# Keys for the estimate of the softmax maximum: column tiles in fp32 over 16 keys a head, against the whole array in fp32r over 32

## The chip, the cores and the metric

The kernel runs on one core of a Trainium2 chip. The metric is the time of one execution on the device in microseconds; of the kernel before, three runs gave 940.66 us (median; 939.57 to 941.91). The profile is one further execution of the same program. In it PE is TensorE's matmul, PEld its weight load, DVE VectorE, ACT ScalarE, POOL GpSimd and SP SyncE.

## The reference

For 2048 tokens of width 448 the reference mixes, by a gate for each token, an attention branch (16 heads of 28, one shared set of keys and values) and an MLP branch that shifts tokens against each other.

```
g = sigmoid((x * gate_w).sum(-1))
q = (x @ wq) in 16 heads of 28;  k = x @ wk;  v = x @ wv
p = softmax(q @ k.T * 28 ** -0.5)          # over all 2048 keys
a = (p @ v, heads side by side) @ wo
h  = gelu(layernorm(x) @ w1), its four quarters shifted by +1, -1, +2, -2 tokens
x1 = x + h @ w2
b  = x1 + gelu(layernorm(x1) @ w3) @ w4
out = g * a + (1 - g) * b
```

A softmax has the same value whatever number is taken off all scores of a row, as long as no exponential overflows. The kernel uses that: it takes off not the maximum over all 2048 keys, but the maximum over the first few.

## The kernel before

The kernel works in three stages: projections and the shifted mixing (to about 165 us), the w3/w4 MLP (to 401 us), and attention with the output projection (to the end). All five engines take their instructions in the order in which the code is written; nothing is sorted afterwards.

The attention stage is cut into 16 units. Unit u holds four heads (their 28 query rows lie at partitions 0, 32, 64 and 96) of one block of 512 tokens. A unit has eight steps (`i` from 0 to 7), each over two tiles of 128 keys. In one step the instructions of TensorE stand in this order:

- twelve score products for the first key tile, then twelve for the second (L204, in `scores`). Each works on a row tile of the array, 32 rows x 128 columns, and streams 512 queries as fp32r; four of them, one a head, run side by side. The results go to two single PSUM banks and a bank pair for each key tile.
- the value products of the step before (L868, in `values`): column tiles of 128 rows x 32 columns, fp32, four side by side, one a head. They write to the bank `s0`, and, where the step has no other use for it, in two halves to `s0` and `s1`.
- in most steps one or two parts of the output projection (L820, in `by_columns`): column tiles in fp32 as well, 224 columns each.

ScalarE takes the exponentials of the single banks and of the pairs (L857). VectorE copies one pair out of PSUM (L905), adds the values to the sum of the unit (`values_end`, L794) and adds the output projection (L839). The second score group of a step can begin only when the two single banks that the previous step used as `s0` and `s1` are read.

The maxima of the next unit are made in step `i = 2` of a unit (`at_max`, `MAX_AT = 2`), in place of the output projection: the values go whole to `s0`, and `max_part` writes its products to `s1`. There are fifteen such steps, for units 1 to 15. In `max_part` (L206) the stationary operand is the 128 queries of a token tile `t` (all four heads, 128 rows), and the moving operand is `khd`, in which the first `MK` keys stand four times on a block diagonal, so that one product gives `MK` scores for each of four heads. One `reduce_max` on VectorE (L213) then makes 16 maxima for each partition. `max_end`, two steps later, splits them and sends them by DMA into spare rows of the queries, where the score products subtract them.

Unit 0 has its maxima made during the MLP stage: four calls of `max_part`, one token tile each, are dealt out as `fills` between the w4 products (L683 to L685, whole array, fp32r, 448 columns) of block 2.

At the end of the kernel, `check` looks whether a row's sum of exponentials went above `LIMIT` = 1e18; if one did, a branch computes all of attention again with true maxima (`max_full`).

Of the kernel before, what the change touches and what calls it, by code (L numbers as in the profile page):

```python
# [9 lines left out]
F32 = mybir.dt.float32  # L10
F32R = mybir.dt.float32r
# [5 lines left out]
P = 128  # L17
# [12 lines left out]
EPS = 1e-5  # L30
SHIFTS = (-1, 1, -2, 2)
PB = 6
MK = 32
LIMIT = 1e18


def f32(ap):
    return ap.bitcast(F32)
# [3 lines left out]
def gated_mix_kernel(  # L42
# [12 lines left out]
    nc = tc.nc  # L55
# [98 lines left out]
    def layernorm_stats(pool, b):  # L154
        mv, rs = stats_tiles(pool, b)
        for t in range(4):
            stats_tile(pool, b, t, mv)
        stats_end(mv, rs)
        return mv, rs

    def layernorm_norm(b, t, mv, rs, xn, xt4):
        xt = x1[:, 4 * b + t, :]
        nc.vector.tensor_scalar(xn, xt, mv[:, t, 0:1], rs[:, t:t + 1], op0=ALU.subtract, op1=ALU.mult)
        nc.vector.transpose(xt4[:, :, t, :], xn.rearrange("p (f j) -> p f j", j=32))
# [3 lines left out]
    def xt_write(b, xt4):  # L168
        xd_of[b] = dram.tile([NE, 32, 4, 128], F32, tag="xd", bufs=2, name=f"xd_{b}")
        for p in range(4):  # L170
            nc.sync.dma_start(xd_of[b][:, :, p].rearrange("f i u -> i f u"),
                              xt4[32 * p:32 * p + 32].rearrange("i f t j -> i f (t j)"))
# [9 lines left out]
    qr_of, qh_of, ql_of = {}, {}, {}  # L182
# [8 lines left out]
    def q_high(u, qh, ql):  # L191
        qh_of[u], ql_of[u] = qh, ql
        nc.vector.tensor_copy(qh, qr_of[u])
# [12 lines left out]
    def max_part(u, ts, ps):  # L206
        if u not in mx_of:
            mx_of[u] = late.tile([P, 4, 4], F32, tag="mr", bufs=2, name=f"mr_{u}")
        n = len(ts)
        for i, t in enumerate(ts):  # L210
            nc.tensor.matmul(ps[:, i * 4 * MK:(i + 1) * 4 * MK], qh_of[u][:, t * P:(t + 1) * P], khd,
                             start=True, stop=True)
        nc.vector.reduce_max(mx_of[u][:, :, ts[0]:ts[0] + n].rearrange("p j t -> p t j"),  # L213
                             ps[:, 0:n * 4 * MK].rearrange("p (t j k) -> p t j k", t=n, j=4), axis=AX.X)

# [34 lines left out]
    with tc.tile_pool(name="s1b", bufs=1) as s1b, \  # L250
# [319 lines left out]
        s1_stack.close()  # L570

        late = ctx.enter_context(tc.tile_pool(name="late", bufs=1, side="right", reuse_waits="tile"))
        khd = late.tile([P, 4 * MK], F32R, name="khd")
        kh_of.append(late.tile([P, S], F32R, name="kh"))
        qh0 = late.tile([P, 512], F32R, name="qh0")
        ql0 = late.tile([P, 512], F32R, name="ql0")
# [7 lines left out]
        def big(name):  # L584
            return s2a.tile([P, 2048], F32, tag="big", bufs=2, name=name)

        def load_w34(i, pool):
            w3h.append(pool.tile([P, 4, 2 * P], F32R, name=f"w3h_{i}"))
            w3l.append(pool.tile([P, 4, 2 * P], F32R, name=f"w3l_{i}"))
            w4h.append(pool.tile([P, 2, D], F32R, name=f"w4h_{i}"))  # L590
            w4l.append(pool.tile([P, 2, D], F32R, name=f"w4l_{i}"))
            raw = big(f"w34raw_{i}")
            raw3[i] = raw[:, 0:1024].rearrange("p (c n) -> p c n", c=4)
            raw4[i] = raw[:, 1024:1024 + 2 * D].rearrange("p (c n) -> p c n", c=2)
            nc.sync.dma_start(raw3[i], w3[:, :, i * 256:i * 256 + 256])
            nc.sync.dma_start(raw4[i], w4[i * 256:i * 256 + 256, :].rearrange("(c p) n -> p c n", p=P))

        def split_w3(i):
            split_w(raw3[i], w3h[i], w3l[i])

        def split_w4(i):
            nc.scalar.copy(w4h[i], raw4[i])
            nc.vector.tensor_tensor(w4l[i], raw4[i], f32(w4h[i]), ALU.subtract)
# [3 lines left out]
        def ln_read(b):  # L607
            xraw2[b] = big(f"xr_{b}").rearrange("p (c n) -> p c n", c=4)
            xt_read(b, xraw2[b])
# [40 lines left out]
    with tc.tile_pool(name="s2", bufs=1, reuse_waits="tile") as s2, \  # L650
            tc.tile_pool(name="ps2", bufs=1, space=PSUM, reuse_waits="tile") as ps2:
        def weigh_x1(n0, n1):
            for n in range(n0, n1):
                nc.gpsimd.tensor_scalar(x1[:, n, :], x1[:, n, :], gi[:, n:n + 1], None, op0=ALU.mult)
# [4 lines left out]
        def fill():  # L659
            if fills:  # L660
                fills.pop(0)()

        def w3_part(b, f):
            i, k = divmod(f, 2)
            ps = mm_tile(f"g_{b}_{f}")
            proj(ps, w3h[i][:, :, k * P:(k + 1) * P], w3l[i][:, :, k * P:(k + 1) * P], *acts[b])
            if (b, f) == (NB - 1, NF - 1):
                nc.scalar.activation(gf_late, ps, AF.Gelu_apprx_tanh)
                return None
            gh = s2.tile([P, 512], F32R, tag="gh", bufs=3, name=f"gh_{b}_{f}")  # L670
            gl = s2.tile([P, 512], F32R, tag="gl", bufs=3, name=f"gl_{b}_{f}")
            gf = s2.tile([P, 512], F32, tag="gf", bufs=1, name=f"gf_{b}_{f}")
            nc.scalar.activation(gh, ps, AF.Gelu_apprx_tanh)  # L673
            nc.scalar.activation(gf, ps, AF.Gelu_apprx_tanh)  # L674
            nc.vector.tensor_sub(gl, gf, f32(gh))  # L675
            return gh, gl
# [10 lines left out]
        for b in range(NB):  # L687
            acc = [ps2.tile([P, 512], F32, tag="acc", bufs=4, name=f"acc_{b}_{t}") for t in range(4)]
            gs = {}
            for f in range(NF):  # L690
                if f == 9 and b + 1 < NB:
                    mv, rs = layernorm_stats(s2a, b + 1)
                if f == 10 and b + 1 < NB:
                    xt4 = big(f"xt4_{b + 1}")[:, 0:4 * D].rearrange("p (f t j) -> p f t j", f=NE, t=4)
                if f in (10, 11) and b + 1 < NB:
                    for t in (2 * f - 20, 2 * f - 19):
                        xn = s2a.tile([P, 512], F32, tag="xn", bufs=1, name=f"xn_{b + 1}_{t}")[:, 0:D]
                        layernorm_norm(b + 1, t, mv, rs, xn, xt4)
                if f == 11 and b + 1 < NB:
                    xt_write(b + 1, xt4)  # L700
                    ln_read(b + 1)
                gs[f] = w3_part(b, f)
                if b == 0 and f % 2 and f < 11:
                    split_w3((f + 3) // 2)
                    split_w4((f + 3) // 2)
                    if f < 9:
                        load_w34((f + 5) // 2, s2)
                if b == 1 and f == 0:
                    nc.gpsimd.tensor_tensor(gg, invE, gz, ALU.pow)
                    nc.vector.tensor_scalar(gg, gg, 1.0, None, op0=ALU.add)  # L710
                    nc.vector.reciprocal(gg, gg)
                    nc.vector.tensor_scalar(gi, gg, -1.0, 1.0, op0=ALU.mult, op1=ALU.add)
                if b == NB - 1 and f == 4:
                    weigh_x1(0, 4 * b)
                if b == 1 and f == 1:
                    nc.gpsimd.memset(f32(khd), 0.0)
                    for j in range(4):
                        h = slice(32 * j, 32 * j + DH)
                        nc.gpsimd.tensor_copy(khd[h, j * MK:(j + 1) * MK], f32(kh_of[0])[h, 0:MK])
                    qr0 = s2a.tile([P, 512], F32, tag="xn", bufs=1, name="qr_0")  # L720
                    nc.gpsimd.memset(qr0, 0.0)
                    q_load(0, qr0)
                    nc.sync.dma_start(w4_late, w4[F - P:F, :])
                if b == 1 and f == 5:
                    q_high(0, qh0, ql0)
                    q_low(0)
                if f >= 2:
                    for t in range(4):
                        w4_part(f - 2, t, gs[f - 2], acc)
                        if b > 1 and t % 2 == 0 and f < NF - 1:  # L730
                            fill()
            for t in range(4):
                w4_part(NF - 2, t, gs[NF - 2], acc, NF - 2 if b == NB - 1 else NF - 1)
                if b + 1 < NB:
                    ln_split(b + 1, t, t + 1)
            for t in range(4):
                if b < NB - 1:
                    w4_part(NF - 1, t, gs[NF - 1], acc)
                xt = x1[:, 4 * b + t, :]
                nc.vector.tensor_add(xt, xt, acc[t][:, 0:D])  # L740
# [5 lines left out]
    with tc.tile_pool(name="s3", bufs=1, reuse_waits="tile") as s3, \  # L746
# [150 lines left out]
        for c in range(NC):  # L897
            u, i = divmod(c, NT // 2)
# [62 lines left out]
        u = NU - 1  # L961
# [84 lines left out]
        with tc.If(again > 0, label="redo"):  # L1046
            for b in range(NB):
                for g in range(NG):
                    u = b * NG + g
# [6 lines left out]
                    for kt in range(NT):  # L1056
                        ps = [bank(f"s2_{u}_{kt}_{j}") for j in range(4)]
# [4 lines left out]
                        for j in range(4):  # L1062
                            nc.tensor.matmul(pv[32 * j:32 * j + 32, :], vext[:, kt, :], p[:, j],
                                             start=(kt == 0), stop=(kt == NT - 1), tile_position=(0, 32 * j))
# [3 lines left out]
                    for t in range(4):  # L1068
                        ps = bank(f"wo2_{u}_{t}")[:, whole]
# [53 lines left out]
```

## Time and profile before

| | |
|---|---|
| median of three runs | 940.66 us (939.57 to 941.91) |
| profiled execution: time, span | 941.63 us, 939.8 us |
| granted TensorE clock | 0.999 |
| TensorE products of the maxima | 64 (60 in attention, 4 in the MLP stage) |
| reductions of the maxima | 15 of 128 x 512, 4 of 128 x 128 |
| attention stage | from about 401 us to the end |

The time of an execution is the span (first to last instruction) and a little around it, here 1.8 us. A row of the timeline gives start, time to the end, engine, line, operation, the tiles out<-in, and how many instructions are merged; in brackets stands for how long the engine was idle before, and what it waited for. Two shapes are given for a matmul: rows x columns of the stationary operand, and partitions x columns of the moving one. A matmul's end is modelled and lies behind the moment at which the next group can start, so paces are read from starts.

### The profile page before, as it was taken

The numbers are of one execution on the slowest core, as the hardware profiler recorded it, in microseconds if no ns is written. First come the engines' busy times: TensorE is split into PE (matmuls) and PEld (weight loads), VectorE is DVE, ScalarE is ACT, GpSimd is POOL, SyncE is SP. The second block draws the span as 40 slices with busy tenths as digits, with TensorE's granted clock in tenths as the row PEclk, the third lists the DMA queues.
The fourth block names the chain that finished last, engine by engine and source line by source line (L and its number), as shares of the span: only waits on it lengthen the run. The fifth ranks groups of instructions, "written<-read, shape, count | busy, mean of one in ns | idle before, by whom it ended". The sixth has DMA issues, their size and how long they took to land.

```text
span 939.8 us, 22620 instructions
## 1 busy us (share of the span) xinstructions
PE 924.7 (98%) x9573; PEld 618.8 (66%) x9573; DVE 516.5 (55%) x922; ACT 637.4 (68%) x1006; POOL 81.6 (9%) x111
## 2 busy tenths in 40 slices
PE   9999999999999999999999999999999999999997
PEld 6788888888888888855555555555555555555552
DVE  3664264531432431166766666666666666766664
ACT  5542444332222222279999999999999999999994
POOL 3343420200000520020000000000000000000000
PEclk9999999999999999999999999999999999999999
DMA  9822552220300300020000010000011000010001
GB/s 310 288 76 56 168 162 91 50 54 1 84 1 1 84 1 0 1 60 18 19 14 24 13 44 34 24 13 15 23 43 34 15 23 13 27 50 10 8 14 43
DMA packets 40435, 47.24 MB, mean 50 GB/s; under 512 B 10120, under 2 KB 28488, under 8 KB 40328
## 3 DMA queue, kind: packets, MB, share of 16 engines
q1 hardware_dynamic: 37304, 40.27, 14.5%
q10 hardware_dynamic: 3024, 5.47, 1.6%
q8 instruction: 76, 1.25, 0.6%
q14 instruction: 31, 0.25, 0.1%
HBM read 32.56 MB, written 11.67 MB: 47 GB/s over the span
## 4 chain that ended last, share of the span: by engine, by line
PE 92%; ACT 4%; DMA 1%; issue 1%; DVE 1%; SPq 0%; POOL 0%; ACTq 0%; DVEq 0%
PE bank L868 24%; PE bank L204 18%; PE bank L820 5%; PE acc L683 5%; PE acc L685 5%; PE acc L684 5%; ACT p L857 4%; PE g L135 4%; PE g L136 4%; PE g L137 4%; PE pair L204 2%; PE hs L461 1%; PE hs L462 1%; PE g L138 1%; PE g L139 1%; PE h L135 1%
## 5 line engine op out<-in xcount | busy, mean ns | idle before, releaser
L857 ACT ACTIVATE p<-bank 128x512 f32<-128x512 f32 x512 | 265.2, 607 | 25.0 <-PE pair L204 13.9
L868 PE MATMUL bank<-p,vext 128*32 128x256 f32 (+1 forms) x3520 | 245.3, 415 | 4.7 <-ACT p L857 1.3
L868 PEld LDWEIGHTS bank<-p,vext 128*32 128x32 f32 x3520 | 101.4, 109 | 125.8 <-ACT p L857 57.5
L905 DVE COPY p<-pair 128x1024 f32<-128x1024 f32 x127 | 155.5, 1225 | 47.9 <-PE pair L204 39.1
L673 ACT ACTIVATE gh<-g 128x512 fp32r<-128x512 f32 x55 | 32.9, 598 | 183.9 <-PE g L139 183.9
L794 DVE TENSOR_TENSOR o<-o,bank 128x256 f32<-128x256 f32 (+1 forms) x188 | 88.2, 469 | 109.3 <-PE bank L868 76.7
L857 ACT ACTIVATE p<-p 128x1024 f32<-128x1024 f32 x127 | 139.2, 1096 | 0.0
L857 ACT ACTIVATE p<-pair 128x1024 f32<-128x1024 f32 x129 | 136.8, 1060 | 0.0
L675 DVE TENSOR_TENSOR gl<-gf,gh 128x512 fp32r<-128x512 f32 x55 | 38.3, 696 | 166.4 <-ACT gf L674 166.4
L204 PE MATMUL bank<-qh,kh 32*128 32x512 f32 x512 | 125.5, 449 | 0.2 <-DVE ot L839 0.2
L204 PE MATMUL pair<-qh,kh 32*128 32x512 f32 x512 | 118.1, 457 | 0.3 <-DVE x L740 0.3
L204 PE MATMUL bank<-ql,kh 32*128 32x512 f32 x512 | 111.0, 394 | 0.0
L204 PE MATMUL bank<-qh,kl 32*128 32x512 f32 x512 | 108.7, 389 | 0.0
L204 PE MATMUL pair<-ql,kh 32*128 32x512 f32 x512 | 101.0, 389 | 0.0
L204 PE MATMUL pair<-qh,kl 32*128 32x512 f32 x512 | 100.9, 388 | 0.0
L204 PEld LDWEIGHTS bank<-qh,kh 32*128 32x128 f32 x512 | 54.0, 182 | 63.3 <-issue 21.9
L683 PE MATMUL acc<-w4h,gh 128*128 128x448 f32 x220 | 80.3, 365 | 0.0
L685 PE MATMUL acc<-w4h,gl 128*128 128x448 f32 x220 | 80.0, 364 | 0.0
L684 PE MATMUL acc<-w4l,gh 128*128 128x448 f32 x220 | 80.0, 363 | 0.0
L820 PE MATMUL bank<-wof,on 128*32 128x224 f32 (+1 forms) x992 | 67.6, 359 | 0.0
L135 PE MATMUL g<-ah,w3h 128*128 128x512 f32 x168 | 65.8, 392 | 0.0
L136 PE MATMUL g<-al,w3h 128*128 128x512 f32 x168 | 65.7, 391 | 0.0
(199 smaller groups left out, 1418.7 us busy)
## 6 DMA issues: line engine op xcount, KB each, us to landing
qd<-qf ACTq DMA_DIRECT2D x16, 256.0 KB
rb<-rd SPq DMA_DIRECT2D x15, 256.0 KB
x<-in_x_dram SPq DMA_DIRECT2D x4, 896.0 KB
xd<-xt SPq DMA_DIRECT2D x16, 224.0 KB
w34raw<-in_w_dram SPq DMA_DIRECT2D x7, 512.0 KB
qr<-qd SPq DMA_DIRECT2D x64, 56.0 KB
out_dram<-ot SPq DMA_DIRECT2D x15, 224.0 KB
w34raw<-in_w_dram SPq DMA_DIRECT2D x7, 448.0 KB
```

The costliest lines, as they stand in the source:

```text
L135: nc.tensor.matmul(ps, wh[:, c, :], ah[:, c, :], start=(c == 0), stop=False)
L136: nc.tensor.matmul(ps, wh[:, c, :], al[:, c, :], start=False, stop=False)
L204: nc.tensor.matmul(ps[j], k[h, keys], q[h, :], start=(r == 0), stop=(r == 2), tile_position=(32 * j, 0))
L675: nc.vector.tensor_sub(gl, gf, f32(gh))
L683: nc.tensor.matmul(ps, gh[:, tok], w4h[i][:, k, :], start=(f == 0), stop=False)
L684: nc.tensor.matmul(ps, gh[:, tok], w4l[i][:, k, :], start=False, stop=False)
L685: nc.tensor.matmul(ps, gl[:, tok], w4h[i][:, k, :], start=False, stop=(f == stop))
L794: nc.vector.tensor_add(o, o, pv)
L820: nc.tensor.matmul(ps[32 * i:32 * i + 32, :], a[:, c:c + 32], w, start=True, stop=True, tile_position=(0, 32 * i))
L857: nc.scalar.activation(p[:, heads], p[:, heads] if source is None else source, AF.Exp, scale=SCALE)
L868: nc.tensor.matmul(pv[32 * j:32 * j + 32, :], vext[:, kt, :], p_of[k][:, j, qs], start=(k == ks[0]), stop=(k == ks[-1]), tile_position=(0, ...
L905: nc.vector.tensor_copy(pa[:, both], pairs[0])
```

## The change

`MK` goes from 32 to 16, so `khd` has 64 columns instead of 128 and a reduction reads half as many scores. In `max_part` each product of 128 x 128 by 128 columns becomes four products of 128 rows x 32 columns by 64 columns, at the four column tiles, each for 32 tokens. `khd` is stored as fp32 instead of fp32r and the queries are read as fp32; the numbers in them are those that were rounded for fp32r before. The copies that fill `khd` on GpSimd become half as wide. Nothing else is touched; from the second hunk on, lines move down by two.

```
-MK = 32
+MK = 16
...
         for i, t in enumerate(ts):
-            nc.tensor.matmul(ps[:, i * 4 * MK:(i + 1) * 4 * MK], qh_of[u][:, t * P:(t + 1) * P], khd,
-                             start=True, stop=True)
+            for c in range(4):
+                m = t * P + 32 * c
+                nc.tensor.matmul(ps[32 * c:32 * c + 32, i * 4 * MK:(i + 1) * 4 * MK], f32(qh_of[u])[:, m:m + 32], khd,
+                                 start=True, stop=True, tile_position=(0, 32 * c))
...
-        khd = late.tile([P, 4 * MK], F32R, name="khd")
+        khd = late.tile([P, 4 * MK], F32, name="khd")
...
-                    nc.gpsimd.memset(f32(khd), 0.0)
+                    nc.gpsimd.memset(khd, 0.0)
```

On TensorE, in step 2 of unit 0, before the change. `bank_0` and `bank_1` are this step's `s0` and `s1`, `p_0_2` and `p_0_3` the exponentials of key tiles 2 and 3, `qh_1` the queries of unit 1, `qh0` those of unit 0, `kh` the keys; the shape is that of the result:

```order
L868 MATMUL bank_0_3223<-p_0_2_3306,vext_74 32x512 [waits Activation_49]
L868 MATMUL bank_0_3223<-p_0_2_3306,vext_74 32x512 x3
L868 MATMUL bank_0_3223<-p_0_3_3330,vext_74 32x512 x4
L211 MATMUL bank_1_3224<-khd_1043,qh_1_3310 128x128 [waits Activation_49]
L211 MATMUL bank_1_3224<-khd_1043,qh_1_3310 128x128 x3
L204 MATMUL bank_2_3225<-qh0_1045,kh_1044 128x512 [waits Activation_49]
```

The same place after the change:

```order
L870 MATMUL bank_0_3235<-p_0_2_3318,vext_74 32x512 [waits Activation_49]
L870 MATMUL bank_0_3235<-p_0_2_3318,vext_74 32x512 x3
L870 MATMUL bank_0_3235<-p_0_3_3342,vext_74 32x512 x4
L213 MATMUL bank_1_3236<-khd_1043,qh_1_3322 32x64 [waits Activation_49]
L213 MATMUL bank_1_3236<-khd_1043,qh_1_3322 32x64 x15
L204 MATMUL bank_2_3237<-qh0_1045,kh_1044 128x512 [waits Activation_49]
```

Four products became sixteen at the same place, with the same wait; they now have the tile shape of the value products ahead of them.

On TensorE, in block 2 of the MLP stage, before the change (`acc_2_0` and `acc_2_1` are the sums of two token tiles, `m_0_0` the bank for the scores of the first token tile):

```order
L684 MATMUL acc_2_0_2286<-w4l_0_1056,gh_2_0_2302 128x448
L685 MATMUL acc_2_0_2286<-w4h_0_1055,gl_2_0_2303 128x448
L211 MATMUL m_0_0_2347<-khd_1043,qh0_1045 128x128
L683 MATMUL acc_2_1_2287<-w4h_0_1055,gh_2_0_2302 128x448
L684 MATMUL acc_2_1_2287<-w4l_0_1056,gh_2_0_2302 128x448
```

The same place after the change:

```order
L686 MATMUL acc_2_0_2286<-w4l_0_1056,gh_2_0_2302 128x448
L687 MATMUL acc_2_0_2286<-w4h_0_1055,gl_2_0_2303 128x448
L213 MATMUL m_0_0_2347<-khd_1043,qh0_1045 32x64 x4
L685 MATMUL acc_2_1_2287<-w4h_0_1055,gh_2_0_2302 128x448
L686 MATMUL acc_2_1_2287<-w4l_0_1056,gh_2_0_2302 128x448
```

Here four column tiles stand between products that use the whole array.

## The prediction

> **What bounds the kernel now.** I read the page first, then a table by stage, then the timeline around one step with maxima. The page's heads and its chain of work:
>
> ```profile
> span 939.8 us, 22620 instructions
> PE 924.7 (98%) x9573; PEld 618.8 (66%) x9573; DVE 516.5 (55%) x922; ACT 637.4 (68%) x1006; POOL 81.6 (9%) x111
> PE 92%; ACT 4%; DMA 1%; issue 1%; DVE 1%; SPq 0%; POOL 0%; ACTq 0%; DVEq 0%
> ```
>
> TensorE carries 92% of the chain, but ScalarE is nearly full in attention. The table by stretches (length, then busy time of PE, PEld, DVE, ACT, POOL) has the w4 stretch with the four fills, and one attention unit:
>
> ```profile
> 262.00:282.00 20.00, 20.00 (x96) 17.40 (x95) 6.39 (x13) 4.35 (x8) 0.00 (x0) 1.00 0.00 1
> 499.30:531.90 32.60, 32.36 (x492) 17.35 (x488) 22.20 (x40) 31.42 (x50) 0.00 (x0) 1.00 0.07 18
> ```
>
> In the MLP stretch TensorE has no gap. In a unit of 32.6 us ScalarE is idle for 1.2 us, so up to that much can be taken from TensorE before ScalarE bounds. The operations that change (least/median/greatest ns):
>
> ```profile
> L211 PE MATMUL bank<-khd,qh x60: 272/275/328, 414.5 to 870.2; 128*128 128x128 f32 x60
> L213 DVE TENSOR_REDUCE mr<-bank x15: 683/685/686, 415.3 to 870.7; 128x16 f32<-128x512 f32 x15
> L213 DVE TENSOR_REDUCE mr<-m x4: 283/288/294, 274.4 to 279.8; 128x4 f32<-128x128 f32 x4
> ```
>
> The timeline of step 2 of unit 0 and the start of step 3 (unit 0's first step with maxima; the others are within 0.02 us of it):
>
> ```profile
> 413.57 1.04 PE L868 MATMUL bank<-p,vext 128*32 128x512 f32 x8
> ...
> 414.00 0.61 PE L868 MATMUL bank<-p,vext 128*32 128x512 f32 x4
> 414.55 0.52 PEld L211 LDWEIGHTS bank<-khd,qh 128*128 128x128 f32 x4 [0.84 <-ACT p L857]
> ...
> 414.74 0.69 DVE L794 TENSOR_TENSOR o<-o,bank 128x512 f32<-128x512 f32 x1 [1.40 <-PE bank L868]
> 414.87 1.09 ACT L857 ACTIVATE p<-p 128x1024 f32<-128x1024 f32 x1
> 415.14 0.18 PEld L204 LDWEIGHTS bank<-qh,kh 32*128 32x128 f32 x2
> ...
> 415.35 0.68 DVE L213 TENSOR_REDUCE mr<-bank 128x16 f32<-128x512 f32 x1
> ...
> 415.94 0.64 PE L204 MATMUL bank<-qh,kh 32*128 32x512 f32 x2
> 416.08 0.18 PEld L204 LDWEIGHTS bank<-qh,kh 32*128 32x128 f32 x1 [0.19 <-DVE mr L213]
> ...
> 416.19 1.09 ACT L857 ACTIVATE p<-bank 128x512 f32<-128x512 f32 x2 [0.23 <-PE pair L204]
> ...
> 416.99 0.13 PEld L868 LDWEIGHTS bank<-p,vext 128*32 128x32 f32 x4 [0.37 <-ACT p L857]
> ```
>
> Two things cost time here. The maxima hold TensorE from 414.55 to the next score load at 415.14. Then the second score group of step 3, which could start at 415.94, stands until 416.08, because its bank is still being read by the reduction. That load sets the next values: 416.99, 0.91 us behind it. The wait is named for all fifteen units:
>
> ```profile
> PEld bank L204 <- DVE mr L213: 2.9, 15, 0.2
> ```
>
> **Step with maxima, TensorE.** Nearest rows for fp32 column tiles of few columns: the values with 256 columns and the projection with 224, one step later.
>
> ```profile
> 418.52 0.40 PE L868 MATMUL bank<-p,vext 128*32 128x256 f32 x4
> ...
> 418.74 0.56 PE L820 MATMUL bank<-w_late,gf_late 128*32 128x224 f32 x8
> ...
> 418.93 0.37 PE L820 MATMUL bank<-w_late,gf_late 128*32 128x224 f32 x4
> ...
> 419.23 0.18 PEld L204 LDWEIGHTS bank<-qh,kh 32*128 32x128 f32 x2 [0.36 <-ACT p L857]
> ...
> 420.94 0.16 PEld L868 LDWEIGHTS bank<-p,vext 128*32 128x32 f32 x8 [0.49 <-ACT p L857]
> ```
>
> Four side by side take 0.216 us for 256 columns (418.52 to 418.74) and 0.19 for 224: 0.84 ns a column, so 64 columns take 0.054. From the last four to the score load is 0.30 (418.93 to 419.23), of which 0.19 is their stream; 0.11 is the change of tile shape. Before the change there are two such changes around the maxima: values to whole array, and whole array to row tiles. After it, the first is gone, since the values have the same tiles. The last four values start at 414.00 and stream 0.43 (the step from 413.57), so the sixteen products can start at 414.43, and the score load follows at 414.43 + 4 x 0.054 + 0.11 = 414.76: 0.38 earlier than 415.14. This supposes that loads hide behind products, as in L820, where the second four loads cost nothing. If every group showed its load (at most the 0.11 that one load lasts, from a PEld row below) it would be 415.20, 0.06 later than now; the gain below would then be 0.08 us a unit, 1.2 us in all. I take the first, from the same form.
>
> **The same step, VectorE.** The reduction stands behind the addition of the values (414.74 to 415.35), which waits for the values and not for the maxima; so it still starts at 415.35. From 288 ns for 128 columns and 685 for 512 a column costs 1.034 ns and the rest 156; 256 columns take 420 ns. It ends 0.265 us earlier, and the waiting score load moves from 416.08 to 415.82. TensorE itself would be there at 415.94 - 0.38 = 415.56: so the reduction still decides, and 0.12 of the 0.38 is lost in the wait for it. The values of step 3 then start 0.91 later, at 416.73 instead of 416.99. The other bound, the first exponential of the step, lies at 414.76 + 1.71 (419.23 to 420.94 in a plain step) = 416.47. ScalarE can follow: its last exponential of step 2 starts at 414.87 and lasts 1.09, to 415.96; the first of step 3, which found its scores at 416.19 before, finds them at 415.81 and starts 0.15 later than it could, still early enough for values at 416.73.
>
> The gain is 0.265 us a unit, fifteen times: 3.97 us. It holds for any length of the sixteen products that puts the score load at 415.02 or earlier (then 415.02 + 1.71 = 416.73). What is late next is the reduction.
>
> **The fills.** The rows at the first fill, and the one place where products on the whole array are followed by another tile shape; and a column-tile load:
>
> ```profile
> 272.91 0.36 PE L685 MATMUL acc<-w4h,gl 128*128 128x448 f32 x1
> 273.11 0.22 PE L211 MATMUL m<-khd,qh 128*128 128x128 f32 x1
> 273.17 0.42 PE L683 MATMUL acc<-w4h,gh 128*128 128x448 f32 x1
> 273.43 0.36 PE L684 MATMUL acc<-w4l,gh 128*128 128x448 f32 x1
> ```
>
> ```profile
> 401.06 0.37 PE L685 MATMUL acc<-w4h,gl 128*128 128x448 f32 x1
> 401.35 0.18 PEld L204 LDWEIGHTS bank<-qh,kh 32*128 32x128 f32 x2 [0.30 <-issue]
> ```
>
> ```profile
> 410.52 0.11 PEld L820 LDWEIGHTS bank<-w_late,gf_late 128*32 128x32 f32 x1 [1.65 <-DVE o L790]
> ```
>
> Now L684 follows L685 by 0.52; two products without a fill take 2 x 0.20, so a fill costs 0.12. After: 272.91 + 0.29 (to the load of another shape, as at 401.06) = 273.20; a load that nothing hides, between 0.03 (32 columns at 0.84 ns) and 0.11, taken as 0.03; products 0.05; change back 0.11: 273.39; the load of L683, also bare, 0.11 (four L211 loads in 0.52, the last 0.19 long, are 0.11 apart): 273.50; and L684 0.20 later, 273.70. That is 0.27 later than now; four times, 1.08 us, all on the path, since nothing but TensorE works without a gap there. Bounds: -0.12 (the fill costs nothing) and +0.45 (both loads and both changes at 0.15), so -0.5 to +1.8 us.
>
> The Trainium skill has a rule for this: "TensorEngine Tiling (Array Packing)", Key Properties, says that changing the tiling mode, not only the tile, drains TensorE. The trace agrees with 0.11 us a change; the rule counts one change less in each of fifteen steps and eight more in the fills, 0.8 us net gained by changes alone.
>
> **At no cost.** 192 more products and loads are issued; no DMA, wait or semaphore is added, and MATMUL order elsewhere stays. GpSimd's filling of `khd` gets shorter at 173 us, where it is not awaited. The fill reductions (288 ns) are hidden in a VectorE that is busy for 6.39 of 20 us. Sixteen keys give lower maxima and larger exponentials; worked out from the reference's inputs the largest row sum is e^25, against e^41 for `LIMIT`, so the branch at the end stays untaken.
>
> **The sum.** -3.97 + 1.08 = -2.89 us. The profiled execution would go from 941.63 to 938.7; it lies 0.97 above the median, and from the median 940.66 the forecast is 937.8, -0.31%. About 0.3% (2.8 us) is also what a measurement can tell from no change, so the forecast stands on that line.
>
> **Rivals.** *TensorE is not fed fast enough.* A plain step has 64 products from 419.23 to the next score load:
>
> ```profile
> 423.19 0.18 PEld L204 LDWEIGHTS bank<-qh,kh 32*128 32x128 f32 x2 [0.36 <-issue]
> ```
>
> That is 62 ns a product, and I found no step that goes below it. If that is a floor, sixteen products take 0.99 us, the score load comes at 415.53, the values at 417.24 (+1.71), 0.25 later: +3.75 us; and in a fill four take 0.25 instead of 0.05, so 0.46 each, +1.85. Time 946.3, slower. It decides from 40 ns a product on: there the score load is at 415.18, the values at 416.89, and 15 x 0.10 pays just for four fills of 0.38. Against it: the eight projection products come in fours 0.19 apart, 47 ns each, and the second four loads were not late. Chance 0.12. The Trainium skill, "TensorE: Matmul & The Clock Gate", section "Wait — 56ns, not 53.3ns?", knows such floors: about 25 ns from start to start, or 62 ns a matmul where the sequencer decodes in microcode. By 62 the time is this rival's; by 25 the score load is at 414.94 and the sum stays as it is but for about 0.2 us in the fills.
>
> *The unit gives the gain back.* Another engine holds the rest of the unit, ScalarE first: then the fills alone are left, 941.7. Its idle 1.2 us a unit is 4.5 times the gain; chance 0.12.
>
> *The reduction does not hold.* If the whole 0.38 arrives, 15 x 0.38 - 1.08 = 4.6 us: 936.0. It would need a reduction of 0.30 us; chance 0.10.
>
> **How the numbers follow.** The forecast's mechanism has 0.66; being on the line, 0.54 of that lies beyond 0.3% and the rest within. Faster: 0.36 + 0.10 = 0.46. Same: 0.30 + 0.12 = 0.42. Slower 0.12. The range goes from 935.7, a little past the last rival, to 942.2, past the second and the upper bound of the fills (+1.8 - 3.97 = -2.2, so 938.5); the slow rival stays out.
>
> **What would show it.** Score load 0.38 us earlier behind the last values; a reduction of 0.42 us that starts at the same distance behind them; the named wait of the score load on the reduction still there, about as long or longer (2.9 us to some 4 us); the values of step 3 0.26 us earlier; L684 0.79 us behind L685 at the fills. Wrong would be: sixteen products longer than 0.6 us, or units whose length stays at 32.6.

## The result and the profile after

The changed kernel takes 938.36 us (median of 12 runs, 936.95 to 939.47), the kernel before, run beside it, 941.46 us (12 runs): a ratio of 0.9971, 95% interval 0.9963 to 0.9979. It is faster by 0.29%.

The page of the profile after, its span, engines and chain:

```profile
span 935.1 us, 23558 instructions
PE 920.3 (98%) x10021; PEld 619.8 (66%) x10021; DVE 512.2 (55%) x922; ACT 637.0 (68%) x1006; POOL 81.4 (9%) x111
PE 93%; ACT 4%; DMA 1%; issue 1%; DVE 1%; SPq 0%; POOL 0%; ACTq 0%; DVEq 0%
```

The two spans (939.8 and 935.1) differ by more than the medians, and most of that excess has nothing to do with the change. The last w4 product ahead of the first fill, up to which the two programs do the same work, starts at 272.91 us before and at 271.36 after (a row below): 1.55 us of it are there before the change begins to act. So I compare stretches. From this w4 product to the first score load of attention: 128.44 us before, 129.78 after, 1.33 longer. Step 1 of unit 0, which waits for the queries by DMA: 5.67 and 4.97; over all runs below it lies between 4.93 and 5.67, whatever the change. From step 2 of unit 0 to the score load of the last step: 509.06 and 505.22, 3.84 shorter. The two stretches that the change touches give 1.33 - 3.84 = -2.5 us, against -2.7 us by the ratio.

The operations that changed (count, least/median/greatest ns):

```profile
L213 PEld LDWEIGHTS bank<-khd,qh x480: 110/110/111, 413.1 to 865.6; 128*32 128x32 f32 x160
L213 PE MATMUL bank<-khd,qh x480: 218/219/220, 413.5 to 865.7; 128*32 128x64 f32 x160
...
L215 DVE TENSOR_REDUCE mr<-bank x15: 418/419/421, 414.4 to 866.2; 128x16 f32<-128x256 f32 x15
```

The reduction takes 0.419 us, from 0.685. The products are 480 records (rows of the trace) where the program has 15 x 16 = 240: an fp32 product is two records.

The timeline of step 2 and the start of step 3 of unit 0, as it was shown of before:

```profile
412.65 1.04 PE L870 MATMUL bank<-p,vext 128*32 128x512 f32 x8
413.08 0.61 PE L870 MATMUL bank<-p,vext 128*32 128x512 f32 x4
...
413.51 0.63 PE L213 MATMUL bank<-khd,qh 128*32 128x64 f32 x32
413.82 0.69 DVE L796 TENSOR_TENSOR o<-o,bank 128x512 f32<-128x512 f32 x1 [1.40 <-PE bank L870]
...
414.07 0.18 PEld L204 LDWEIGHTS bank<-qh,kh 32*128 32x128 f32 x2
...
414.42 0.42 DVE L215 TENSOR_REDUCE mr<-bank 128x16 f32<-128x256 f32 x1
...
414.87 0.53 PE L204 MATMUL bank<-qh,kh 32*128 32x512 f32 x2
414.89 0.18 PEld L204 LDWEIGHTS bank<-qh,kh 32*128 32x128 f32 x1
...
415.12 0.60 ACT L859 ACTIVATE p<-bank 128x512 f32<-128x512 f32 x1
...
415.79 0.14 PEld L870 LDWEIGHTS bank<-p,vext 128*32 128x32 f32 x5 [0.37 <-ACT p L859]
```

Counted from the start of the last four values (413.08; before 414.00): the products start 0.43 behind it, with no change of shape between; the score load comes at 0.99 (before 1.14); the reduction starts at 1.34 as before (1.35); the awaited load of the second score group comes at 1.81 (2.08); and the values of step 3 at 2.71 (2.99). A unit (median of units 1 to 14, between the score loads of their first steps) goes from 32.56 to 32.30 us: 0.26.

The first fill after:

```profile
271.36 0.37 PE L687 MATMUL acc<-w4h,gl 128*128 128x448 f32 x1
271.66 0.32 PE L213 MATMUL m<-khd,qh 128*32 128x64 f32 x8
271.91 0.47 PE L685 MATMUL acc<-w4h,gh 128*128 128x448 f32 x1
272.21 0.37 PE L686 MATMUL acc<-w4l,gh 128*128 128x448 f32 x1
```

The second product behind the fill comes 0.85 us behind L687, from 0.52: 0.33 a fill, 1.3 us in four, which is the 1.33 of the stretch.

### The profile page after: what moved, and what is told of

Same layout as the page of the kernel before. It is cut to its first block, busy times and chain, and to the rows that moved or that the text cites. A ratio compares the mean times of both kernels' runs of the same rounds, so it can differ in the third digit from the quotient of the medians.

```text
span 935.1 us, 23558 instructions
## 1 busy us (share of the span) xinstructions
PE 920.3 (98%) x10021; PEld 619.8 (66%) x10021; DVE 512.2 (55%) x922; ACT 637.0 (68%) x1006; POOL 81.4 (9%) x111
## 3 DMA queue, kind: packets, MB, share of 16 engines
HBM read 32.56 MB, written 11.67 MB: 47 GB/s over the span
## 4 chain that ended last, share of the span: by engine, by line
PE 93%; ACT 4%; DMA 1%; issue 1%; DVE 1%; SPq 0%; POOL 0%; ACTq 0%; DVEq 0%
PE bank L870 25%; PE bank L204 18%; PE bank L822 5%; PE acc L685 5%; PE acc L687 5%; PE acc L686 5%; PE g L135 4%; PE g L136 4%; PE g L137 4%; ACT p L859 4%; PE pair L204 1%; PE hs L463 1%; PE hs L464 1%; PE g L138 1%; PE g L139 1%; PE h L135 1%
## 5 line engine op out<-in xcount | busy, mean ns | idle before, releaser
L687 PE MATMUL acc<-w4h,gl 128*128 128x448 f32 x220 | 80.1, 364 | 0.0
```

The source lines that it names most:

```text
L687: nc.tensor.matmul(ps, gl[:, tok], w4h[i][:, k, :], start=False, stop=(f == stop))
```

## The experiments

Theory A is the prediction's reckoning of step 3, with the sizes that the trace after shows: its values start at the later of two bounds, the score load + 1.71 us (the first exponential of the step) and the end of the reduction + 0.95 us (0.05 to the load of the second score group, 0.90 from there). Rival B: the reduction alone decides. Rival C: TensorE's own time, the score load, alone decides. The expectations count from the last of the last four values, 0.02 us later than the table below. Ratios are to the kernel before, run on the same chip. No run has column tiles in fp32r, so "tiles" below always means the tile shape together with fp32.

**Keys alone: 16 keys, whole array, fp32r.**

```
-    def max_part(u, ts, ps):
+    def max_part(u, ts, ps, whole=True):
...
+            if whole:
+                nc.tensor.matmul(ps[:, i * 4 * MK:(i + 1) * 4 * MK], qh_of[u][:, t * P:(t + 1) * P], khd,
+                                 start=True, stop=True)
+                continue
             for c in range(4):
...
-        khd = late.tile([P, 4 * MK], F32, name="khd")
+        khd = late.tile([P, 4 * MK], F32R, name="khd")
```

> Only the number of keys changes (16 a head); the products stay on the whole array in fp32r. All times from the start of the last four values of step 2, as the traces have them: before, score load 1.11 and values of step 3 at 2.955; after, 0.97 and 2.69. Theory A: the values of step 3 start at the later of two bounds, score load + 1.71 and end of the reduction + 0.95. Here the score load comes at 1.09 (four loads of 0.11 still set the pace, only the last stream is shorter) and the reduction ends at 1.74 as after: values at 2.80, set by the score load. That is 0.155 us a unit, 2.3 us, and about 0.1 from the fills, which keep their tile shape: 2.4 us faster than before. Rival B, the reduction alone decides: values at 2.69, 15 x 0.265 + 0.1 = 4.1 us faster. Rival C, TensorE's own time alone decides: 15 x 0.02 + 0.1 = 0.4 us faster.

Measured: 0.9965 (0.9953 to 0.9977), 3.3 us faster than before; the interval, 2.2 to 4.4 us, holds the 2.4 of A and the 4.1 of B, so the trace decides. The timeline of the same step:

```profile
412.89 0.61 PE L874 MATMUL bank<-p,vext 128*32 128x512 f32 x4
...
413.43 0.64 PE L212 MATMUL bank<-khd,qh 128*128 128x64 f32 x4
...
413.99 0.18 PEld L204 LDWEIGHTS bank<-qh,kh 32*128 32x128 f32 x2
...
414.23 0.42 DVE L219 TENSOR_REDUCE mr<-bank 128x16 f32<-128x256 f32 x1
...
415.69 0.14 PEld L874 LDWEIGHTS bank<-p,vext 128*32 128x32 f32 x5 [0.47 <-ACT p L863]
```

The four loads still hold TensorE, the score load comes at 1.10, and the values at 2.80, although the reduction is as short as after. A unit is 32.40 us, 0.16 shorter than before: A (0.155), not B (0.265) or C (0.02). The fills cost what they did: the second product behind one still comes at 0.52 us. By the clock this kernel can't be told from the one with tiles: what tiles win in attention they lose in the fills.

**Tiles alone: 32 keys, column tiles, fp32.** `MK = 32` in the kernel after, nothing else.

> Only the tiles change: column tiles in fp32, 32 keys a head as before (128 columns a product). If each fp32 product runs as two passes, there are eight groups of 0.109 us: score load at 0.41 + 0.87 + 0.11 = 1.39, 0.28 later than before. The products end too late for the reduction to start at 1.32; it starts at about 1.58, ends at 2.27, values of step 3 at 3.22 instead of 2.955: 15 x 0.265 = 4.0 us slower, and the fills cost 0.33 + 0.11 more each, 1.75: 5.7 us slower than before. If a product were one pass (four groups, as the prediction reckoned): score load at 0.96, reduction as before, and only the fills are left: about 1.3 us slower.

Measured: 1.0065 (1.0052 to 1.0077), 6.1 us slower.

```profile
415.64 0.61 PE L870 MATMUL bank<-p,vext 128*32 128x512 f32 x4
...
417.05 0.18 PEld L204 LDWEIGHTS bank<-qh,kh 32*128 32x128 f32 x2 [0.20 <-issue]
...
417.34 0.69 DVE L215 TENSOR_REDUCE mr<-bank 128x16 f32<-128x512 f32 x1 [0.28 <-PE bank L213]
...
418.99 0.14 PEld L870 LDWEIGHTS bank<-p,vext 128*32 128x32 f32 x5 [0.36 <-ACT p L859]
```

The score load comes at 1.41: eight groups of four, two records a product. VectorE now waits 0.28 us for the products, and the reduction starts 0.1 later than I expected (1.70), so the values come at 3.35. So tiles pay only with few columns, while fewer keys gain without tiles too (above).

**8 keys in column tiles.** `MK = 8` in the kernel after.

> As after, with 8 keys a head (32 columns a product, reduction over 128 columns, 0.288 us). Theory A, if a group of 32 columns takes half of 0.056: score load at 0.76, its bound 2.47; reduction ends at 1.61, its bound 2.56: values at 2.56, 15 x 0.395 = 5.9 us, less fills of 4 x 0.27: 4.8 us faster than before. Theory A, if the weight load keeps a group at 0.056: score load 0.97, values at 2.68, 2.8 us faster, as after. Rival B (the reduction alone decides): 4.8 us faster in both cases. Which case it is, the distance of the groups in the timeline shows.

Measured: 0.9962 (0.9949 to 0.9975), 3.6 us faster than before, where A said 4.8.

```profile
414.68 0.61 PE L870 MATMUL bank<-p,vext 128*32 128x512 f32 x4
...
415.11 0.48 PE L213 MATMUL bank<-khd,qh 128*32 128x32 f32 x32
...
415.52 0.18 PEld L204 LDWEIGHTS bank<-qh,kh 32*128 32x128 f32 x2
...
416.02 0.29 DVE L215 TENSOR_REDUCE mr<-bank 128x16 f32<-128x128 f32 x1
...
417.26 0.14 PEld L870 LDWEIGHTS bank<-p,vext 128*32 128x32 f32 x5 [0.36 <-ACT p L859]
```

Attention did as A said for short groups, and B says the same here: values at 2.58, a unit 32.18 us, 0.39 shorter than before. The first seven groups start 0.03 us apart, near the half of 0.056; in the last two the records come singly, up to 17 ns apart, so that the score load follows the first product by 0.41 us, from 0.56 with 16 keys. What is missing was lost outside attention: the w3 products of the MLP stage (first and last start; `x168` are all blocks) stretch over 271.4 us, against 268.4 before and 269.7 after. Two kernels at the end of this section test why.

```profile
L135 PE MATMUL g<-ah,w3h x168: 389/393/398, 124.9 to 396.2; 128*128 128x512 f32 x168
```

**A shorter reduction alone.** The kernel after; the reduction reads 8 of the 16 scores of each head.

```
-                             ps[:, 0:n * 4 * MK].rearrange("p (t j k) -> p t j k", t=n, j=4), axis=AX.X)
+                             ps[:, 0:n * 4 * MK].rearrange("p (t j k) -> p t j k", t=n, j=4)[:, :, :, 0:8], axis=AX.X)
```

> As after, products and all, but the reduction reads only the first 8 of the 16 scores of each head (128 of 256 columns, 0.288 us instead of 0.419); the result stays the same softmax with another subtracted maximum. Theory A: the reduction's bound goes from 2.69 to 2.56, but the score load stays at 0.97, and its bound is 2.68: values at 2.68, less than 0.2 us in all against after; about 2.8 us faster than before. Rival B (the reduction alone decides): values at 2.56, 15 x 0.13 = 2.0 us faster than after, 4.7 faster than before.

Measured: 0.9960 (0.9947 to 0.9973); its interval holds both answers, so the trace decides.

```profile
413.04 0.61 PE L870 MATMUL bank<-p,vext 128*32 128x512 f32 x4
...
414.03 0.18 PEld L204 LDWEIGHTS bank<-qh,kh 32*128 32x128 f32 x2
...
414.38 0.28 DVE L215 TENSOR_REDUCE mr<-bank 128x16 f32<-128x128 f32 x1
...
415.08 0.60 ACT L859 ACTIVATE p<-bank 128x512 f32<-128x512 f32 x1
...
415.73 0.14 PEld L870 LDWEIGHTS bank<-p,vext 128*32 128x32 f32 x5 [0.46 <-ACT p L859]
```

The reduction is 0.13 us shorter and the values come at 2.69 instead of 2.71; a unit is 32.285 instead of 32.30. B falls. The first exponential (415.08 to 415.68) now ends right ahead of the values at 415.73.

The two bounds against what was measured in unit 0, in us from the start of the last four values:

| kernel | score load | + 1.71 | reduction ends | + 0.95 | values of step 3 |
|---|---|---|---|---|---|
| before | 1.14 | 2.85 | 2.03 | 2.98 | 2.99 |
| after | 0.99 | 2.70 | 1.76 | 2.71 | 2.71 |
| 16 keys, whole array | 1.10 | 2.81 | 1.76 | 2.71 | 2.80 |
| 32 keys, tiles | 1.41 | 3.12 | 2.39 | 3.34 | 3.35 |
| 8 keys, tiles | 0.84 | 2.55 | 1.63 | 2.58 | 2.58 |
| reduction over 8 of 16 | 0.99 | 2.70 | 1.62 | 2.57 | 2.69 |

The later of the two comes within 0.01 us of the values in all six. In the kernel after the bounds are 0.01 apart.

**Fills on the whole array, attention as after.** `max_part` takes a flag; the fills call it with the product in the old shape (64 columns, fp32r). `khd` is stored as fp32r again, and the column tiles read it as fp32.

```
+            if whole:
+                nc.tensor.matmul(ps[:, i * 4 * MK:(i + 1) * 4 * MK], qh_of[u][:, t * P:(t + 1) * P], khd,
+                                 start=True, stop=True)
+                continue
```

> As after in attention, but the four fills of the MLP stage keep the whole array in fp32r (with 64 columns). If the fills cost what their rows say (second product behind L687 at 0.85 us after, 0.52 before), they go back to 0.52, 4 x 0.33 = 1.3 us faster than after, and the units stay at 32.30 us: about 4.0 us faster than before. If the delay of the fills is made good later in the MLP stage, the time is that of after, 2.7 faster than before.

Measured: 0.9952 (0.9934 to 0.9971), 4.5 us faster than before; the interval, 2.7 to 6.2 us, reaches down to the second answer, so the trace decides.

```profile
271.72 0.36 PE L691 MATMUL acc<-w4h,gl 128*128 128x448 f32 x1
271.92 0.19 PE L212 MATMUL m<-khd,qh 128*128 128x64 f32 x1
271.95 0.45 PE L689 MATMUL acc<-w4h,gh 128*128 128x448 f32 x1
272.24 0.36 PE L690 MATMUL acc<-w4l,gh 128*128 128x448 f32 x1
```

0.52 us again, and 128.44 us from the w4 product ahead of the first fill to attention, to the hundredth what it was before the change, against 129.78 after: nothing later in the MLP stage makes the delay of the fills good. Units stay at 32.29.

**Products between the two key tiles of the values.** The reduction then stands ahead of the addition of the values on VectorE.

```
-        def values(ks, pv, qs=slice(0, 512)):
+        def values(ks, pv, qs=slice(0, 512), between=None):
             for k in ks:
+                if between and k == ks[-1]:
+                    between()
...
-                values((k - 2, k - 1), s0)
+                if at_max:
+                    values((k - 2, k - 1), s0, between=lambda: max_part(u + 1, range(4), s1))
+                    later.append(lambda u=u: max_end(u + 1))
+                else:
+                    values((k - 2, k - 1), s0)
                 values_end(v, s0)
                 if at_max:
-                    max_part(u + 1, range(4), s1)
-                    later.append(lambda u=u: max_end(u + 1))
+                    pass
```

> As after, but the sixteen products stand between the value products of the two key tiles (still one run of column tiles), and the reduction stands ahead of the addition of the values on VectorE. The reduction is then long over when its bank is wanted; the addition of the values now ends last. Theory A with that bank put in: the last values start 0.45 later than in after, the addition ends 1.43 behind them, its bank is loaded at 1.47 and the next values come at 2.37; counted as in after 2.82 instead of 2.70: 0.12 a unit, 1.8 us slower than after. Rival: the reduction was the only thing waited for on VectorE; then the values come at score load + 1.71, 2.72 counted as in after, and the time is that of after within 0.3 us.

Measured: 0.9980 (0.9970 to 0.9991), so some 0.8 us slower than after, though the two intervals overlap; the units decide.

```profile
415.48 0.61 PE L872 MATMUL bank<-p,vext 128*32 128x512 f32 x4
...
416.02 0.18 PEld L204 LDWEIGHTS bank<-qh,kh 32*128 32x128 f32 x2 [0.84 <-ACT p L859]
...
416.90 0.18 PEld L204 LDWEIGHTS bank<-qh,kh 32*128 32x128 f32 x2 [0.34 <-DVE o L796]
...
417.80 0.14 PEld L872 LDWEIGHTS bank<-p,vext 128*32 128x32 f32 x5 [0.36 <-ACT p L859]
```

The wait moved from the reduction to the addition of the values, as A with that bank says, but the load came at 1.42 and not at 1.47: 0.06 us a unit instead of 0.12 (32.36 against 32.30). The order on VectorE that the kernel has is the better one.

**8 keys and fills on the whole array.** Both edits above.

> The two gains together: 8 keys a head in column tiles in attention (values of step 3 0.13 us earlier than after, as measured with 8 keys), fills on the whole array (0.52 instead of 0.85). Theory A: units of 32.17 us and fills at 0.51: 15 x 0.395 + 0.1 = 6.0 us faster than before, 3.3 faster than after. If the unit gave part of it back to ScalarE: between 4 and 6 us faster than before.

Measured: 0.9956 (0.9937 to 0.9976), 4.1 us faster: short of the 6.0. Units have 32.17 us and the fills cost 0.51, as expected. But the MLP stage is longer. The w3 products, first with 16 keys and fills on the whole array, then with 8:

```profile
L135 PE MATMUL g<-ah,w3h x168: 388/392/398, 125.6 to 394.1; 128*128 128x512 f32 x168
```

```profile
L135 PE MATMUL g<-ah,w3h x168: 387/393/398, 127.1 to 397.4; 128*128 128x512 f32 x168
```

By the starts in nanoseconds, 268.41 us against 270.26. In the second, w3 products of neighbouring `f` (the 128-wide slices of the hidden layer, in the order of the code) stand 4.92 to 5.04 us apart instead of 4.89 to 4.97 wherever no fill stands between them, in every block, so also before any product of the maxima has run. The w3 and w4 instructions are the same; what differs is that a smaller key tile moves the tiles allocated behind it on its side of the memory by 128 bytes a partition. This follows from the code; the traces hold no addresses. The next two kernels test it.

**8 keys, key tile kept at 64 columns.**

```
-        khd = late.tile([P, 4 * MK], F32R, name="khd")
+        khd = late.tile([P, 64], F32R, name="khd")[:, 0:4 * MK]
```

> As the kernel with 8 keys and fills on the whole array, but the tile that holds the keys keeps 64 columns (256 bytes a partition), of which 32 are used, so that all tiles behind it stand where they stand in after. If the place of the tiles makes the MLP stage of the two kernels with 8 keys slow (4.99 us instead of 4.96 or 4.92 between the w3 products of neighbouring f, 1.8 us from the first to the last), the stage goes back from 268.86 to 267.02 us, attention keeps its 32.17 us a unit, and the time is 15 x 0.395 = 5.9 us below before. Rival, the smaller maxima themselves cost it: the stage stays at 268.9, about 4.1 us below before.

Measured: 0.9939 (0.9925 to 0.9953), 5.7 us faster than before: 936.01 us, the lowest median here (the interval overlaps that of 16 keys with fills on the whole array).

```profile
L135 PE MATMUL g<-ah,w3h x168: 388/392/398, 127.0 to 395.4; 128*128 128x512 f32 x168
```

268.41 us again.

**The kernel after, key tile widened to 96 columns.**

```
-        khd = late.tile([P, 4 * MK], F32, name="khd")
+        khd = late.tile([P, 96], F32, name="khd")[:, 0:4 * MK]
```

> As after, but the tile that holds the keys has 96 columns, of which 64 are used: the same work, all tiles behind it stand 128 bytes further. If the place of the tiles is the cause: the MLP stage goes from 268.35 to about 270.1 us, units stay at 32.30, 1.8 us slower than after. Rival, the place has no part in it: the stage at 268.35, the time that of after.

Measured: 0.9992 (0.9983 to 1.0001), 2.0 us slower than after. The w3 products after, and in this kernel:

```profile
L135 PE MATMUL g<-ah,w3h x168: 388/392/398, 125.3 to 395.0; 128*128 128x512 f32 x168
```

```profile
L135 PE MATMUL g<-ah,w3h x168: 389/393/398, 125.1 to 396.6; 128*128 128x512 f32 x168
```

269.74 us against 271.57: the same work, 128 bytes further, costs 1.8 us, two thirds of what the whole change gains. The place of the tiles is the cause; which tile's place it is was not tried. All eleven traces fit: the three kernels with a key tile of 128 or 384 bytes a partition have the distances of 4.92 to 5.04 us, the eight with 256 or 512 bytes those of 4.89 to 4.97.

## Why the prediction was right

The time lies 0.6 us above the forecast of 937.8, and the forecast's -0.31% lies within the interval of the ratio. The mechanism, a shorter reduction in attention against dearer fills, is the one that acted; one term of it was off by a factor of two, and that this did no harm is luck. By its steps:

- *What bounds.* Right: TensorE in both stages. ScalarE did not take the gain back; units got 0.26 us shorter, so the second rival falls.
- *The reduction.* Right: 420 ns forecast, 419 measured, with the same start. The gain of 0.265 us a unit is the measured one (2.08 - 1.81 = 0.27 at the awaited load).
- *Sixteen products.* Mis-sized: "the score load follows at 414.43 + 4 x 0.054 + 0.11 = 414.76: 0.38 earlier" measured 0.15 earlier. I took the eight L820 records for eight products. The code issues four (one call of `by_columns`), so each fp32 product is two records; sixteen products are eight groups, 0.056 apart (0.45 us), not four. The Trainium skill states in "FP8 and Floating Point Precision", TensorE Precision Notes, that true FP32 takes four passes through the array. The trace agrees in time: two records of 0.84 ns a column make 1.68 ns, 3.7 times the 0.45 ns of fp32r (512 columns in 0.23 us). Of the 0.15, 0.12 is the change of shape that is gone (the maxima start 0.43 behind the last values instead of 0.55); from there to the score load it is 0.56 us, from 0.59.
- *Why that did no harm.* Luck. The forecast held for a score load at 415.02 or earlier and reckoned with 414.76, 0.26 in hand; measured by the same clock it came at 414.99. The margin was 0.03 us there, and the reduction decided by 0.01 (the table). A little later and the score load would have decided, as it does with 16 keys on the whole array.
- *The fills.* Forecast 0.79 us behind the w4 product, measured 0.85; the missing 0.06 fits the second group of records, 0.056, that the forecast left out. That is 1.3 us instead of 1.08, and the kernel with fills on the whole array shows that all of it reaches attention.
- *The named wait.* Wrong: I expected the score load's wait on the reduction to stay, some 4 us in all. It is not among the named waits any more. The load still comes 0.05 us behind the end of the reduction (414.89 and 414.84), but the first product of its group starts only at 414.87, so the reduction holds TensorE by 0.02 us, from 0.14 before (415.94 to 416.08). That is the 0.38 again: with it the forecast had a wait of 0.26.
- *The rival "not fed fast enough".* Refuted: the sixteen products take 0.45 us, 28 ns each, below the 40 from which it would decide. Its 62 ns was a price of records too: the 64 rows of the plain step are 44 products, and a record takes 14 ns here. Of the two floors that the Trainium skill gives in "TensorE: Matmul & The Clock Gate", section "Wait — 56ns, not 53.3ns?", neither the 62 ns nor the 25 ns shows between the records here, where four tiles run side by side.
- *The rival "the reduction does not hold".* Its price was wrong with the 0.38: what TensorE saved was 0.15, and the kernel with the shorter reduction finds 0.02 us a unit behind it, not 0.12.

In the sum, 3.97 us forecast as gained and 1.33 lost give 2.6; the stretches measured 3.84 and 1.33, 2.5, and the ratio 2.7.

## What to carry to other kernels

Before a price is taken from a merged row, count what the code issues against what the row counts; here a factor of two hid in "x8". Column tiles cost little behind products of the same shape and 0.33 us more a fill in a stream of whole-array products, so one helper called from both places can win in one and lose in the other: let the caller choose the shape. And when a small tile changes its size, pad it to the old size once, to see whether the move of its neighbours is part of what was measured.

## What the hardware showed that was not expected

A shift by 128 bytes a partition of the tiles behind `khd` lengthens the w3/w4 products of the whole MLP stage by 1.8 us of some 269 (0.7%), at equal instructions and a granted clock of 0.997 to 0.999, and padding takes it away (268.41 and 270.26, 269.74 and 271.57 us above). The mean distance of w3 products within a run of them grows from 228.8 to 230.5 ns. Before and after, whose key tiles have 512 and 256 bytes, show no such difference. Why is open.

Column-tile products of 64 columns run at 0.056 us for a group of four records side by side, two groups for four products; their loads of 0.11 us are hidden behind the groups ahead. At 32 columns the first groups come 0.03 us apart, but the last two do not keep that pace, so there something other than the columns begins to count; what it is was not tried.
